# Transposing the attention probabilities as float32r from score buffers at a fixed place

## The chip, the cores and the metric

The kernel runs on one core of one Trainium2 chip. What counts is the device time of one execution in microseconds. Each number of the tables is the median of several executions; the rows of the trace come from one further, profiled execution.

## The reference

Four batches of eight heads, a sequence of 576, a head of 64, all in float32, followed by two feed-forward layers over 2304 tokens (512 to 2048 to 512):

```python
scores = scale * np.matmul(q, k.transpose(0, 1, 3, 2))
cum = np.cumsum(np.maximum(s, 0.0), axis=-1)
bias = -(cum[:, :, :, None] - cum[:, :, None, :])
scores = np.where(causal, -1000000000.0, scores + np.minimum(bias, 0.0))
attn = np.exp(scores - np.max(scores, axis=-1, keepdims=True))
attn = attn / (np.sum(attn, axis=-1, keepdims=True) + 1e-09)
x = np.matmul(attn, v)                  # then (tokens, heads * head_dim)
h = x @ w_in1;  x = np.maximum(0.01 * h, h) @ w_out1
h = x @ w_in2;  x = (np.maximum(h, 0.0) + np.log1p(np.exp(-np.abs(h)))) @ w_out2
```

The feed-forward weights come as float64 and are split in the kernel.

## The kernel before, in words

Three stages follow each other: attention (about the first 240 us) with a part of the first feed-forward layer woven in, the rest of the first layer, and the second layer. In both layers each float32 operand is split into two float32r tiles, a high and a low part, and a product is three float32r matmuls (lines 145, 635, 854, 1023, 1078, 1105).

Attention works on 16 pairs of heads. The 576 query rows of a pair are cut into units: the block of rows 384 to 511, a unit called "last" for the remaining 64 rows of both heads, the block of rows 256 to 383, and the two first blocks together. A unit passes through a pipeline, one step of the main loop behind the other:

- `scores`: TensorE multiplies Q and K in float32 and adds the decay bias through a second matmul of two rows (lines 302, 307, 316), into two PSUM tiles, j = 0 and 1 for the two heads;
- `maxima`: VectorE (DVE) adds the mask, finds the row extremes and writes the scores into `sc`, a tile of 128 x 2 x 512 float32 from a ring of three buffers (line 337);
- `exps`: ScalarE (ACT) takes the exponential in place and its row sums (line 349);
- `norm`: GpSimd (POOL) multiplies by the reciprocal of the sum in place (line 360);
- `transpose`: TensorE transposes each 128 columns of `sc` into a PSUM tile `pt_t`, with the identity `ident` as the streamed operand (lines 368, 372, 377). There are 20 transposes of line 377, four of line 372 and one of line 368 in a pair, 400 in all;
- `evacuate`: ACT or DVE copies `pt_t` to PA, PZ or PB (lines 389, 391);
- `pv`: TensorE multiplies by V in float32 (line 409).

In one step of the loop the unit n is at its maxima and exponentials, n - 1 at its norm, n - 2 at its transposes, and n - 3 at its last evacuation. From about 60 us on, each step also holds six matmuls of the first layer, put there by `fill.step`. The order of instructions on every engine is the order in which the program writes them.

Ahead of the loop stands the preparation: `masks()` and `make_identity(nc, ident)` write on POOL; `decay0()` then issues the loads of the first Q and K from ACT's queue, the loads of s and the later Q, K, V and weights from SP's queue, starts 18 warm-up matmuls on TensorE (`wake`, line 191), and computes the cumulative sums of s with ACT and DVE for the bias rows BK0 and BQ0 (lines 210 to 216).

SBUF is handed out by pools; those with `side="right"` grow from the right edge. At that edge stands `edge`, 24 floats; left of it come the pools of the woven-in layer (`Fill`), which are closed after attention.

Of the kernel before, what the change touches and what calls it, by code (L numbers as in the profile page):

```python
# [10 lines left out]
F32 = mybir.dt.float32  # L11
I32 = mybir.dt.int32
U32 = mybir.dt.uint32
F32R = mybir.dt.float32r
AF = mybir.ActivationFunctionType
# [3 lines left out]
P = 128  # L19
# [6 lines left out]
def view(t, offset, *dims):  # L26

    return bass.AP(t.tensor, t.offset + offset, [list(t.ap[0])] + [list(d) for d in dims])
# [3 lines left out]
def attn_moe_moe(ctx, tc, q, k, v, s, w1i, w1o, w2i, w2o, out):  # L32
    nc = tc.nc

    B, H, S = s.shape
# [8 lines left out]
    NB = S // P  # L44
    TL = S - NB * P
# [5 lines left out]
    def pool(name, bufs=1, **kw):  # L51
        return tc.tile_pool(name=name, bufs=bufs, **kw)
# [2 lines left out]
    keep = ctx.enter_context(pool("keep"))  # L55
    edge = ctx.enter_context(pool("edge", side="right"))
    edge.tile([P, 24], F32, tag="edge", name="edge")

    xh = keep.tile([P, KD, NT], F32R, tag="xh", name="xh")
    xl = keep.tile([P, KD, NT], F32R, tag="xl", name="xl")  # L60
# [11 lines left out]
    def tick():  # L72
        clock[0] += 1
        for fn, args in todo.pop(clock[0], ()):
            fn(*args)
# [78 lines left out]

    def attention(att, ps, fills):
        ident = att.tile([P, P], F32, tag="ident", name="ident")

# [14 lines left out]
        BK0, BQ0 = view(PB, 0, [1, S]), view(PB, S, [1, ZQ])  # L174
        c0, c1 = (view(PA, i * S, [1, S])[:BH] for i in range(2))
        one = view(V[1], 0, [1, S])
        s0, s1 = (view(att.tile([P, 2, 512], F32, tag="sc", name="sc", bufs=3), 0, [1, S]) for _ in range(2))
        base = att.tile([P, 12], F32, tag="st", name="st", bufs=4)[:, :1]

        def blank(i):  # L180
# [12 lines left out]
        def decay0():  # L193

            pitch = list(s1.ap[0])[0]
            nc.sync.dma_start(
                bass.AP(s1.tensor, s1.offset, [[D * pitch, 2], [1, S]]), bass.AP(s.tensor, s.offset, [[S, 2], [1, S]])
            )
            load(0, "q", nc.scalar)
            nc.sync.dma_start(c0, s.rearrange("b h s -> (b h) s"))  # L200
            load(0, "k", nc.scalar, slice(0, S))
            nc.vector.memset(one[:, :P], 1.0)
            wake(one[:, :P])
            nc.vector.memset(one[:, P:], 1.0)
            nc.vector.memset(base, 0.0)
            for j in range(2):
                nc.vector.memset(base[j * D + 32:j * D + 33], -1.0)
            for i in (1, 0):
                nc.vector.memset(BK[i].bitcast(F32), -1.0)
            nc.vector.tensor_scalar(s0[:1], s1[:1], 0.0, 1.0 / scale, op0=ALU.max, op1=ALU.mult)  # L210
            for y, x in ((s0[D:D + 1], s1[D:D + 1]), (c0, c0)):
                nc.scalar.activation(y, x, AF.Relu, scale=1.0 / scale)
            nc.vector.tensor_tensor_scan(BK0, one, s0, base, op0=ALU.mult, op1=ALU.add)
            nc.scalar.activation(BQ0[32:33, :S], BK0[:1], AF.Copy)
            for c, n, queue in ((slice(0, SB), 0, nc.vector), (slice(S, ZQ), SB, nc.gpsimd)):
                queue.tensor_copy(BQ0[D + 32:D + 33, c], BK0[D:D + 1, n:n + c.stop - c.start])
# [20 lines left out]
        def zeros():  # L237
            nc.gpsimd.memset(PZ[TL:], 0.0)
# [40 lines left out]
        class Unit:  # L279
# [43 lines left out]

            def maxima(self, j):
                if j == 0:
                    self.sc = att.tile([P, 2, 512], F32, tag="sc", name="sc", bufs=3)
                    self.st = att.tile([P, 12], F32, tag="st", name="st", bufs=4)
                    if self.last:
                        self.sc = view(self.sc, 0, [self.W, 2], [1, self.W])
                w = slice(0, self.W)  # L330
                ml = (mask[:, w], maskl)[j] if not self.p else M[self.p % 2][:, j * SH:(j + 1) * SH]
                todo = [(w, ml, j)] if self.last else [
                    (c, mask[:, (NB - 1 - t) * P:], j * len(self.subs) + i) for i, (t, c) in enumerate(self.subs)
                ]
                low = self.stat(0, 0) if self.last and j else 3.0e38
                for c, m, e in todo:
                    nc.vector.tensor_tensor_reduce(  # L337
                        out=self.sc[:, j, c], in0=self.ps[j][:, c], in1=m, scale=-scale, scalar=low,
                        op0=ALU.add, op1=ALU.min, accum_out=self.stat(0, e),
                    )  # L340
# [19 lines left out]
                    nc.gpsimd.tensor_scalar(x, x, self.stat(2, e), 1.0, op0=ALU.mult, op1=ALU.mult)  # L360

            def transpose(self, j):
                sc = self.sc
                pt = ps.tile([P, 512], F32, tag="t", name="pt_t", bufs=2)
                if self.last:
                    sc = view(sc, 0, [1, S])
                    if j:
                        nc.tensor.transpose(pt[:TL, :P], sc[:, NB * P:S], ident)
                        self.outs = PZ[:TL], pt[:TL, :P].rearrange("p (j x) -> p j x", x=TL)
                        return  # L370
                    for c in range(NB):
                        nc.tensor.transpose(pt[:, c * P:(c + 1) * P], sc[:, c * P:(c + 1) * P], ident)  # L372
                    self.outs = PA[:, :, :, P:], pt.rearrange("p (c j x) -> p j c x", j=2, x=TL)
                    return
                n = self.W // P
                for c in range(n):
                    nc.tensor.transpose(pt[:, c * P:(c + 1) * P], sc[:, j, c * P:(c + 1) * P], ident)  # L377
                src = pt[:, :self.W].rearrange("p (c x) -> p c x", x=P)
                if n == NB:
                    self.outs = PA[:, j, :, :P], src  # L380
                else:
                    k = len(self.subs)
                    self.outs = PB[:, j, :, (2 - k) * P:(3 - k) * P], src
# [45 lines left out]
        def masks():  # L429
            nc.gpsimd.memset(s0, 0.0)  # L430
            nc.gpsimd.memset(BQ0, 1.0)
            for j in range(2):
                nc.gpsimd.memset(BQ0[j * D:(j + 1) * D, NB * P + (1 - j) * TL:NB * P + (2 - j) * TL], 0.0)
            nc.gpsimd.memset(mask, 0.0)
            nc.gpsimd.memset(maskl, 0.0)
            d0 = (NB - 1) * P
            nc.gpsimd.affine_select(
                out=mask[:, d0:d0 + P], in_=mask[:, d0:d0 + P], compare_op=ALU.is_ge,
                fill=NEG, base=0, pattern=[[-1, P]], channel_multiplier=1,
            )  # L440
            for r in (0, TL):
                nc.gpsimd.affine_select(
                    out=maskl[r:r + TL, S // 2 - TL:], in_=maskl[r:r + TL, S // 2 - TL:], compare_op=ALU.is_ge,
                    fill=NEG, base=0, pattern=[[-1, TL]], channel_multiplier=1,
                )

        fill = fills()
        masks()
        make_identity(nc, ident)
        zeros()  # L450
        decay0()
        for i in (1, 0):
# [19 lines left out]
        for n in range(len(units) + 3):  # L472
            p, i = divmod(n, len(order))
# [185 lines left out]
    with pool("att") as att:  # L659
        attention(att, psA, make)  # L660
    fill = fills[0]
    while fill.units or fill.rest or todo:
        fill.run()
        tick()
    fill.stack.close()

    acc = ctx.enter_context(pool("accpool")).tile([P, KD, NT], F32, tag="acc", name="acc")
    stages = [ExitStack(), ExitStack()]
# [197 lines left out]
    def at(n, fn, *args):  # L866
        plan.setdefault(n, []).append((fn, args))
# [259 lines left out]
    for n, q in enumerate(quads):  # L1127
        q.at(t)
        if n + 1 < len(quads):
            j = quads[n + 1].sb, quads[n + 1].j  # L1130
# [86 lines left out]
```

## Time and profile before

| | us |
|---|---|
| median of 3 runs | 951.89 |
| lowest and highest | 951.88, 952.91 |
| the profiled execution | 951.81 |
| its span, first to last instruction | 950.0 |

| engine | busy us | share of the span | instructions |
|---|---|---|---|
| TensorE matmul (PE) | 941.3 | 99% | 5173 |
| TensorE weight load (PEld) | 767.3 | 81% | 5173 |
| VectorE (DVE) | 668.0 | 70% | 1294 |
| ScalarE (ACT) | 575.8 | 61% | 1185 |
| GpSimd (POOL) | 564.3 | 59% | 548 |

Matmuls are pipelined: a record of one holds its way through the array, so records of neighbours overlap, and the distance from start to start is what each adds. The loading of a matmul's stationary operand has a record of its own under PEld; in a transpose that is the block to be transposed. A chain is followed back from the last instruction to what released each step.

### The profile page before, as it was taken

Reading aid. Unit: us, or ns where it says so; the run is one execution under the profiler, and the core shown is the slowest. Engines: PE = TensorE matmul, PEld = TensorE weight load, DVE = VectorE, ACT = ScalarE, POOL = GpSimd, SP = SyncE. Lnnn points to the kernel's source line nnn. Section 1 sums busy time; section 2 is a strip of 40 time slices with the busy share of each in tenths; the row PEclk is TensorE's granted clock in tenths of the full one; section 3 lists DMA queues with packets and bytes.
Section 4 is the critical chain, followed back from the end, with each engine's and each line's share of the span. In section 5 each row is a group of like instructions: output and inputs, shape, how many; then the busy total and the mean of one; then the engine's idle time right before and its main releaser. Section 6 shows DMA issues by size and latency. Waiting matters only on the chain.

```text
span 950.0 us, 15346 instructions
## 1 busy us (share of the span) xinstructions
PE 941.3 (99%) x5173; PEld 767.3 (81%) x5173; DVE 668.0 (70%) x1294; ACT 575.8 (61%) x1185; POOL 564.3 (59%) x548
## 2 busy tenths in 40 slices
PE   9999999999999999999999999999999999999998
PEld 6666767777998888888888888888888888888887
DVE  8888656554479798778998745665666666766666
ACT  6888677665566564546555446666656765565563
POOL 7778556444367676657666534755654664555443
PEclk9999999999999999999999999999999999999999
DMA  7453434331665654546476244341415248445402
GB/s 248 148 164 127 144 111 134 119 106 37 215 239 180 229 190 139 173 166 213 132 269 217 102 151 159 115 136 66 153 65 177 89 150 314 135 136 175 134 0 90
DMA packets 79251, 143.61 MB, mean 151 GB/s; under 512 B 7626, under 2 KB 24906, under 8 KB 79172
## 3 DMA queue, kind: packets, MB, share of 16 engines
q1 hardware_dynamic: 78740, 141.87, 44.9%
q8 instruction: 41, 0.67, 0.3%
q10 hardware_dynamic: 432, 0.75, 0.3%
q14 instruction: 38, 0.31, 0.1%
HBM read 109.33 MB, written 33.25 MB: 150 GB/s over the span
## 4 chain that ended last, share of the span: by engine, by line
PE 93%; DVE 3%; POOL 1%; ACT 1%; issue 1%; DMA 0%; SPq 0%; DVEq 0%; POOLq 0%; ACTq 0%
PE ps_h L145 20%; PE ps_out L1078 20%; PE ps_out L854 17%; PE ps_h L1023 16%; PE pt_s L316 4%; PE pt_t L377 3%; PE ps_o L635 3%; PE pt_v L409 3%; PE ps_h L1105 2%; PE pt_s L409 1%; PE pt_t L372 1%; PE pt_s L302 1%; DVE sc L337 1%; POOL sc L360 0%; ACT sc L349 0%
## 5 line engine op out<-in xcount | busy, mean ns | idle before, releaser
L974 POOL TENSOR_TENSOR l<-l,e 128x512 f32<-128x512 f32 x72 | 93.5, 1298 | 161.8 <-DVE e L971 147.5
L151 POOL TENSOR_TENSOR gl<-gf,gh 128x512 fp32r<-128x512 f32 (+2 forms) x68 | 88.7, 1305 | 111.7 <-ACT gh L150 78.5
L360 POOL TENSOR_SCALAR sc<-sc,st 128x512 f32<-128x512 f32 (+4 forms) x160 | 88.4, 563 | 79.2 <-DVE st L356 61.3
L145 PE MATMUL ps_h<-xh,wih 128*128 128x512 f32 (+2 forms) x320 | 119.9, 375 | 0.0
L145 PE MATMUL ps_h<-xh,wil 128*128 128x512 f32 (+2 forms) x320 | 118.1, 369 | 0.0
L145 PE MATMUL ps_h<-xl,wih 128*128 128x512 f32 (+2 forms) x320 | 117.9, 368 | 0.0
L1086 DVE TENSOR_TENSOR acc<-ps_out,acc 128x512 f32<-128x512 f32 (+1 forms) x127 | 86.8, 685 | 42.5 <-PE ps_out L1078 40.0
L1078 PE MATMUL ps_out<-woh,gh 128*128 128x512 f32 x290 | 112.5, 388 | 0.8 <-DVE acc L1086 0.8
L1078 PE MATMUL ps_out<-wol,gh 128*128 128x512 f32 x290 | 112.4, 388 | 0.0
L349 ACT ACTIVATE sc<-sc,st 128x512 f32<-128x512 f32 (+2 forms) x144 | 83.4, 582 | 34.5 <-DVE st L337 28.7
L854 PE MATMUL ps_out<-gh,woh 128*128 128x512 f32 (+2 forms) x272 | 99.2, 365 | 0.3 <-DVE acc L861 0.3
L854 PE MATMUL ps_out<-gh,wol 128*128 128x512 f32 (+2 forms) x272 | 99.1, 364 | 0.0
L854 PE MATMUL ps_out<-gl,woh 128*128 128x512 f32 (+2 forms) x272 | 99.0, 364 | 0.0
L834 ACT ACTIVATE gf<-ps_h 128x512 f32<-128x512 f32 (+2 forms) x68 | 37.1, 546 | 101.4 <-PE ps_h L145 92.7
L984 POOL TENSOR_TENSOR gl<-l,gh 128x512 fp32r<-128x512 f32 x72 | 93.6, 1308 | 3.0 <-ACT gh L980 3.0
L1078 PE MATMUL ps_out<-woh,gl 128*128 128x512 f32 x290 | 88.9, 388 | 0.0
L980 ACT ACTIVATE gh<-l 128x512 fp32r<-128x512 f32 x72 | 45.4, 630 | 66.0 <-POOL l L974 66.0
L1023 PE MATMUL ps_h<-xh,wih 128*128 128x512 f32 x208 | 81.0, 389 | 0.0
L1023 PE MATMUL ps_h<-xl,wih 128*128 128x512 f32 x208 | 81.0, 389 | 0.0
L1023 PE MATMUL ps_h<-xh,wil 128*128 128x512 f32 x208 | 80.9, 389 | 0.0
L337 DVE CUSTOM_DVE_ANT_0 sc<-pt_s,mask 128x512 f32<-128x512 f32 (+3 forms) x129 | 59.2, 483 | 16.2 <-PE pt_t L377 15.4
L145 PEld LDWEIGHTS ps_h<-xh,wil 128*128 128x128 f32 x320 | 60.2, 188 | 9.6
(168 smaller groups left out, 2369.7 us busy)
## 6 DMA issues: line engine op xcount, KB each, us to landing
w2d<-stg SPq DMA_DIRECT2D x88, 256.0 KB
rawi<-in_moe_w_in SPq DMA_DIRECT2D x32, 512.0 KB
rawo<-in_moe_w_out SPq DMA_DIRECT2D x32, 512.0 KB
wih<-w2d SPq DMA_DIRECT2D x64, 256.0 KB
wil<-w2d SPq DMA_DIRECT2D x64, 256.0 KB
woh<-w2d SPq DMA_DIRECT2D x32, 256.0 KB
wol<-w2d SPq DMA_DIRECT2D x32, 256.0 KB
K<-in_k SPq DMA_DIRECT2D x15, 432.0 KB
```

Of the source, the lines that this page charges most:

```text
L145: nc.tensor.matmul(ps, a, b, start=kk == 0 and n == 0, stop=kk == KD - 1 and n == 2)
L151: nc.gpsimd.tensor_tensor(gl, gf, gh.bitcast(F32), op=ALU.subtract)
L337: nc.vector.tensor_tensor_reduce(out=self.sc[:, j, c], in0=self.ps[j][:, c], in1=m, scale=-scale, scalar=low, op0=ALU.add, op1=ALU.min, ac ...
L349: nc.scalar.activation(x, x, AF.Exp, scale=-1.0, bias=self.stat(0, e + self.last), accum_out=self.stat(1, e))
L360: nc.gpsimd.tensor_scalar(x, x, self.stat(2, e), 1.0, op0=ALU.mult, op1=ALU.mult)
L854: nc.tensor.matmul(ps, a, b, start=f == 0 and m == 0, stop=f == G - 1 and m == 2)
L974: nc.gpsimd.tensor_tensor(self.l, self.l, self.e, op=ALU.subtract)
L980: nc.scalar.activation(self.gh, self.l, AF.Copy)
L984: nc.gpsimd.tensor_tensor(self.gl, self.l, self.gh.bitcast(F32), op=ALU.subtract)
L1023: nc.tensor.matmul(self.ps[name], x, y, start=n < 4 and kp == 0 and m == 0, stop=kp == 1 and m == 2, skip_group_check=n >= 4,)
L1078: nc.tensor.matmul(u, a, v, start=m == 0, stop=m == len(ops) - 1)
L1086: nc.vector.tensor_tensor(d[..., w], o[..., w], d[..., w], op=ALU.add)
```

## The change

The three buffers of the `sc` ring are no longer pool tiles. A pool `arena` reserves their 12 KB per partition next to the right edge, and each buffer is addressed there under two names: `sc`, float32, for DVE, ACT and POOL, and `bits`, float32r, for the transposes. The identity gets a float32r copy, `turn`, made by ACT right behind `make_identity`, and the transposes write the PSUM tile as float32r. The arena is closed behind the pools of the woven-in layer.

```diff
+    arena = ExitStack()
+    arena.enter_context(pool("arena", side="right")).tile([P, 3, 2, 512], F32, tag="arena", name="arena")
+    low = (nc.sbuf_usable_end - 4 * 24) // P * P - 3 * 2 * 512 * 4
...
         ident = att.tile([P, P], F32, tag="ident", name="ident")
+        turn = att.tile([P, P], F32R, tag="turn", name="turn")
+        at = lambda nm, i, dt: nc.alloc_sbuf_tensor_at(f"{nm}{i}", [P, 2, 512], dt, offset=low + 4 * 1024 * i).ap()
+        scores = cycle([(at("sc", i, F32), at("bits", i, F32R)) for i in range(3)])
...
-        s0, s1 = (view(att.tile([P, 2, 512], F32, tag="sc", name="sc", bufs=3), 0, [1, S]) for _ in range(2))
+        s0, s1 = (view(next(scores)[0], 0, [1, S]) for _ in range(2))
...
                 if j == 0:
-                    self.sc = att.tile([P, 2, 512], F32, tag="sc", name="sc", bufs=3)
+                    self.sc, self.bits = next(scores)
...
             def transpose(self, j):
-                sc = self.sc
+                sc = self.bits
                 pt = ps.tile([P, 512], F32, tag="t", name="pt_t", bufs=2)
+                out = pt.bitcast(F32R)
                 if self.last:
                     sc = view(sc, 0, [1, S])
                     if j:
-                        nc.tensor.transpose(pt[:TL, :P], sc[:, NB * P:S], ident)
+                        nc.tensor.transpose(out[:TL, :P], sc[:, NB * P:S], turn)
...
                     for c in range(NB):
-                        nc.tensor.transpose(pt[:, c * P:(c + 1) * P], sc[:, c * P:(c + 1) * P], ident)
+                        nc.tensor.transpose(out[:, c * P:(c + 1) * P], sc[:, c * P:(c + 1) * P], turn)
...
                 for c in range(n):
-                    nc.tensor.transpose(pt[:, c * P:(c + 1) * P], sc[:, j, c * P:(c + 1) * P], ident)
+                    nc.tensor.transpose(out[:, c * P:(c + 1) * P], sc[:, j, c * P:(c + 1) * P], turn)
...
         masks()
         make_identity(nc, ident)
+        nc.scalar.activation(turn, ident, AF.Copy)
         zeros()
         decay0()
...
     fill.stack.close()
+    arena.close()
```

## Rows read from the trace of the kernel before

**Rows 1.** The page: span, then TensorE's busy time, share and instructions.

```profile
span 950.0 us, 15346 instructions
...
PE 941.3 (99%) x5173; PEld 767.3 (81%) x5173; DVE 668.0 (70%) x1294; ACT 575.8 (61%) x1185; POOL 564.3 (59%) x548
```

**Rows 2.** Busy time by stretch, 180 to 200 us; after POOL: granted clock, DMA share, GB/s.

```profile
180.00:200.00 20.00, 20.00 (x150) 14.11 (x150) 11.62 (x51) 12.46 (x37) 6.64 (x13) 1.00 0.29 98
```

**Rows 3.** The chain by line in four stretches: 5:24, 24:62, 62:100, 100:240 us.

```profile
by line: PE pt_s L316 34.2%; DMA K<-in_k 21.9%; POOL sc L360 7.4%; POOL wm L123 6.3%; PE pt_s L307 6.2%; PE pt_t L377 5.4%; SPq L247 5.1%; DVE sc L337 5.1%; issue 3.6%; PE pt_s L302 3.4%; DVE wm L120 3.2%; PE pt_t L372 3.1%; SPq L82 2.8%; D
...
by line: PE pt_s L316 24.8%; PE pt_v L409 19.4%; PE pt_t L377 17.7%; POOL wil L133 6.6%; PE pt_t L372 6.3%; POOL sc L360 4.9%; issue 4.1%; PE ps_h L145 3.7%; DVE PA L391 3.6%; DVE sc L337 3.1%; PE pt_s L302 1.7%; POOL M L75 1.5%; DVE st L35
...
by line: PE ps_h L145 26.2%; PE pt_s L316 18.9%; PE pt_t L377 16.1%; PE pt_v L409 15.9%; PE ps_o L635 3.7%; PE pt_s L302 3.4%; POOL wol L133 3.3%; PE pt_t L372 3.1%; DVE st L355 2.1%; DVE PA L391 1.8%; issue 1.8%; DVE sc L337 1.6%; POOL sc 
...
by line: PE ps_o L635 18.0%; PE ps_h L145 13.9%; PE pt_s L316 13.8%; PE pt_t L377 12.3%; PE pt_v L409 9.6%; PE pt_s L409 8.9%; PE pt_t L372 3.8%; PE pt_s L302 3.7%; ACT sc L349 3.1%; DVE sc L337 3.0%; issue 2.1%; DVE xl L420 1.5%; POOL wm L
```

**Rows 4.** The chain through one head pair: start us, us, what.

```profile
177.71 0.59 PE pt_t L377 x4
178.30 1.39 PE ps_o L635 x6
179.68 0.44 PE pt_t L377 x4
...
183.38 0.11 PE pt_t L368
...
187.00 0.48 PE pt_t L377 x3
...
188.87 0.66 PE pt_t L377 x6
...
190.91 0.33 PE pt_t L377 x3
```

**Rows 5.** Matmuls by line and shape: count, busy us, mean ns of one record, idle us.

```profile
L1078 PE MATMUL ps_out<-wol,gh 128*128 128x512 f32 x286 | 111.3, 389 | 0.0
...
L1105 PE MATMUL ps_h<-xh,wil 128*128 128x256 f32 x64 | 18.1, 283 | 0.0
...
L409 PE MATMUL pt_v<-PB,V 128*64 128x128 f32 x128 | 12.8, 279 | 0.0
...
L191 PE MATMUL pt_w<-V 128*128 128x128 f32 x18 | 4.2, 430 | 1.0 <-DVE V L202 1.0
```

**Rows 6.** Loads of the stationary operand by line and shape, columns as above.

```profile
L145 PEld LDWEIGHTS ps_h<-xh,wil 128*128 128x128 f32 x320 | 60.2, 188 | 9.6
...
L377 PEld LDWEIGHTS pt_t<-ident,sc 128*128 128x128 f32 x320 | 36.2, 140 | 16.3 <-POOL sc L360 4.3 <-issue 2.8 <-POOL wol L133 0.9
...
L409 PEld LDWEIGHTS pt_v<-PB,V 128*64 128x64 f32 x256 | 15.9, 137 | 6.3 <-issue 1.7
...
L368 PEld LDWEIGHTS pt_t<-ident,sc 128*64 128x64 f32 x16 | 1.8, 110 | 0.5
```

**Rows 7.** POOL in order of time, the second step on ident: start us, us.

```profile
4.38 1.28 POOL masks.py:199 TENSOR_SCALAR_AFFINE_SELECT ident<-ident 128x128 f32<-128x128 f32 x1
```

**Rows 8.** ACT's queue in order of time, the start.

```profile
0.76 0.38 ACTq L247 DMA_DIRECT2D Q<-in_q  x1
1.17 0.45 ACTq L247 DMA_DIRECT2D K<-in_k  x1
```

**Rows 9.** TensorE in order of time at the start, then the chain there.

```profile
1.04 4.21 PE L191 MATMUL pt_w<-V 128*128 128x128 f32 x18 [1.04 <-DVE V L202]
5.47 1.36 PE L316 MATMUL pt_s<-K,Q 64*128 64x512 f32 x4 [0.21 <-DMA K<-in_k]
...
1.17 4.16 DMA K<-in_k
...
5.47 2.22 PE pt_s L316 x8
```

**Rows 10.** Busy time by stretch, 8 to 10 us; columns as in rows 2.

```profile
8.00:10.00 2.00, 2.00 (x16) 1.12 (x10) 2.00 (x6) 1.80 (x5) 1.79 (x6) 1.00 1.04 387
```

**Rows 11.** Waits of attention: engine and line, releaser, us, times, longest us.

```profile
PEld pt_t L377 <- POOL sc L360: 4.3, 12, 0.6
```

## The prediction

> **What bounds the kernel now.** The page first: TensorE (PE) is busy 99% of the span [rows 1], and the granted clock of an attention stretch is 1.00, the higher level, 2.4 GHz [rows 2]. So time taken from TensorE inside attention can shorten the whole, but only where TensorE is what the next step waits for. For that I read the chain of waits, summed by line, over the four parts of attention [rows 3]. The reader is to see two things. The transposes (pt_t, lines 377 and 372) are on the chain everywhere: 8.5% of 19 us, 24.0% of 38 us, 19.2% of 38 us and 16.1% of 140 us, which is 1.6 + 9.1 + 7.3 + 22.5 = 40.5 us. And the first part has another entry, the load of K, with 21.9%: the start hangs on a transfer, not on TensorE.
>
> How much of all transposing is on the chain? One undisturbed head pair shows its seven groups: 0.59 (and a second group like it, line 372), 0.44, 0.11, 0.48, 0.66 and 0.33 us [rows 4], 3.20 us for 25 transposes; 16 pairs give 51.2 us for 400. So 40.5 of 51.2, or 79%: 316 of the 400 transposes lie where their length counts.
>
> **The change, part by part.**
>
> *The transposes.* Six in a row take 0.66 us, 110 ns each [rows 4]. Two things could set that pace: loading the block to be transposed, and streaming the 128 columns of the identity. The matmuls on float32r tiles give the stream: a record of 512 columns is 389 ns and one of 256 columns 283 ns [rows 5], so a column costs 0.41 ns and 128 columns 53 ns; 110 ns is two such passes. The load of a transpose record shrinks from 140 ns for 128 columns to 110 ns for 64 [rows 6], so 128 columns take 60 ns, which fits beneath the 110 ns. The float32 transpose is therefore set by its two streaming passes. As float32r it should stream once, 53 ns. Then the load sets the pace, and here the trace has no row for the new form: if it loads as the float32 transpose does, 60 ns; if it loads as the float32r weights do, whose records shrink from 188 ns for 128 columns to 137 ns for 64 (a float32 load of the same kind) [rows 6], 102 ns. So the gain lies between 50 and 8 ns for each; if the second pass stays, it is nothing. The two nearest rows pull opposite ways (the same operation, or the same type), so I take the middle, 81 ns, a gain of 29 ns. On the chain: 316 x 29 = 9.2 us. Some of it is lost where another engine is close behind, as the twelve waits of the transposes for POOL's normalisation show (4.3 us) [rows 11]; I keep 8.0 us. The ends: 316 x 50 x 0.87 = 13.7 us and 2.5 us, or nothing.
>
> The Trainium skill ("TensorE: Matmul & The Clock Gate", section "Back-to-back issue gap") gives about 81 ns for a weight load and a 128-column matmul in a stream, and about 131 ns at 512 columns; the trace's six 512-column matmuls in 1.39 us [rows 4] are 232 ns each, so the page does not hold here at the larger size, and at 128 columns no run here shows it yet. By it the chain would lose 316 x 29 ns, the same as the middle that I took from the rows.
>
> *The new identity.* One copy of 128x128 on ACT. Its own length is small; its place is what counts. It is written directly behind the building of ident and ahead of decay0, and ACT works its queue in order. The instruction that it waits for, POOL's second step on ident, runs from 4.38 us for 1.28 us, to 5.66 us [rows 7]. Queued on ACT behind the copy are the loads of the first Q and K, which in the kernel before were issued at 0.76 and 1.17 us [rows 8], then the Relus of the decay and the copy for BQ0. TensorE's first scores wait for K: issue at 1.17 us, 4.16 us to landing, scores at 5.47 us [rows 9]. After: the copy starts at about 5.75 us, the Q issue beside or just behind it, K's issue 0.41 us later, at 6.2 us; K lands at 10.3 us at the earliest, and the scores start at about 10.5 us, 5.0 us later. The Relus and the BQ0 copy slip too, but they have the 4 us in which K travels, so they are hidden by it. DVE, POOL and ACT cannot use the time: their attention work is in order behind these scores. So nothing covers the delay, and what starts at 5.47 us moves as a block.
>
> Two additions. In the old place Q and K had a head start on SP's loads; in the new one they meet them, and the DMA engines are full then (share 1.04 from 8 to 10 us) [rows 10]. If they only get their part of it, K comes up to about 1.2 us later; I take 0.5. And the warm-up matmuls, 18 from 1.04 us for 4.21 us [rows 9], no longer touch the scores: TensorE stands idle from 5.25 to 10.5 us. The warm-up runs 18 matmuls of 128 columns at 430 ns a record, where the later float32 ones of 128 columns take 279 ns [rows 5]; 4.21 us over 18 is twice the 110 ns of two passes, the lower level, 1.2 GHz, and before it TensorE had done nothing. If it is back there when the scores come, the chain's work of the next 4 to 5 us, which begins with 2.22 us of scores on TensorE [rows 9], costs up to 2.5 us more. No row of before shows TensorE idle for 5 us, so the ends are 0 and 2.5; I take 1.5.
>
> The Trainium skill (same page, section "What's actually happening") says that the low clock is the default and activity lifts it, so an idle stretch of this kind would cost; no row of before has one. By it alone the start would cost 7.5 to 8.0 us in place of the 5.5 without a clock loss.
>
> Start: 5.0 + 0.5 + 1.5 = 7.0 us, with ends 5.0 and 8.7.
>
> *The fixed place and the two names.* The same three buffers of 4 KB; no instruction is added or removed by it. The arena sits at the right edge until attention is over, so the pools of the next stage take other addresses. I cost this at nothing: in the attention stretches PE has work queued, and the last transposes are read long before that stage writes there. What could cost: TensorE now reads another name than POOL writes, so a transpose of the first half might wait for the whole buffer (below).
>
> **Sum.** The profiled execution: 951.81 us with a span of 950.0, at the median of the three runs (951.89). 951.8 + 7.0 - 8.0 = 950.8 us.
>
> **The rivals.**
>
> *One streaming pass and the short load (B).* For it: the load row of the very same operation, 60 ns [rows 6]. Against: that row is of the other type. 951.8 + 7.0 - 13.7 = 945.1 us.
>
> *The load of float32r sets the pace (C), on the slower side.* For it: every 128-column float32r load in the trace is 188 ns against the transposes' 140 [rows 6]. Place: each transposing group; price: the gain shrinks to 2.5 us or to nothing, and the start remains. 951.8 + 7.0 - 2.5 = 956.3, to 958.8 us. It decides from a spacing of about 95 ns up, where 316 x 15 x 0.87 = 4 us no longer covers the start.
>
> *The loads are not delayed (D).* If the copy does not stand ahead of them on ACT, the start term falls away: 951.8 - 8.0 = 943.8 us. Against: the loads are the first instructions of ACT's queue now, and the copy is written ahead of them.
>
> *The two names make transposes wait for both halves (E).* The longest such wait now is 0.6 us [rows 11]; it would come where POOL is late. With 5 us over 64 units: about 955.8 us. For it only that the reader's name is another one.
>
> **How the numbers follow.** The forecast (A), 950.8 with its own range of 947 to 954 us, has 0.45; B 0.20; C 0.25; D 0.05; E 0.05. A change under 0.2% (1.9 us, 950.0 to 953.8) can't be told from none in this kernel. Faster: B and D whole and a third of A, 0.40. Slower: C and E and an eighth of A, 0.35. The same: the rest of A, 0.25. The range has to reach B's 945 and C's 958: 943.5 to 958.5 us; outside are the far ends of B, C and D, under 0.2.
>
> **What would show it.** In the trace after: ACT's first work behind the table load is the copy, at about 5.75 us, with the loads of Q and K issued behind it, and the first scores at 10.5 to 11.5 us instead of 5.47; the first scores' records longer than before if the clock fell. Transposes in a row at 81 ns (A), 60 ns (B), 102 to 110 ns (C); their load records at 140 ns or at 188. Attention shorter by 8 us from first score to last. The later stages as long as before. Wrong would make it: a spacing outside 70 to 95 ns, a start that is hidden, or transposes with longer waits for POOL.

## The result, and the profile after

| | us |
|---|---|
| the changed kernel, median of 4 runs | 962.19 (960.77 to 963.04) |
| the kernel before on the same chip, median of 4 runs | 952.37 |
| ratio, 95% interval | 1.0102 (1.0084 to 1.0119) |
| the profiled execution, and its span | 960.77, 959.0 |

The change makes the kernel 1.0% slower, some 9.7 us. The prediction said 950.8 us with a range of 943.5 to 958.5, so the time moved the other way and lies outside the range.

The page after: span, TensorE's busy time, the granted clock in 40 slices, and the chain that ended last by engine.

```profile
span 959.0 us, 15300 instructions
...
PE 934.4 (97%) x5173; PEld 763.6 (80%) x5173; DVE 670.0 (70%) x1294; ACT 575.5 (60%) x1186; POOL 563.8 (59%) x548
...
PEclk7999999999999999999999999999999999999999
...
PE 85%; DVE 5%; POOL 3%; ACT 2%; DMA 2%; issue 1%; SPq 0%; DVEq 0%; ACTq 0%; POOLq 0%
```

The last of these lines in the kernel before:

```profile
PE 93%; DVE 3%; POOL 1%; ACT 1%; issue 1%; DMA 0%; SPq 0%; DVEq 0%; POOLq 0%; ACTq 0%
```

Against [rows 1] TensorE is busy 6.9 us less, as the change should make it, but the span is 9.0 us longer: there are 15.9 us more in which TensorE has nothing to do, and its share of the chain falls from 93% to 85%. The clock row, all 9 in later slices, begins with a 7, so the first slice of 24 us is one place to look.

The start, in order of time (start us, us, what): POOL's second step on ident and the ACT queue behind it, then two steps of the chain, then TensorE. The last two lines are of the kernel before: DVE's scan beside POOL's step, and its first transposes.

```profile
4.41 0.29 POOL masks.py:199 TENSOR_SCALAR_AFFINE_SELECT ident<-ident 128x128 f32<-128x128 f32 x1
4.73 0.31 ACT L457 ACTIVATE turn<-ident 128x128 fp32r<-128x128 f32 x1 [2.73 <-POOL ident masks.py:199]
4.74 0.38 ACTq L253 DMA_DIRECT2D Q<-in_q  x1
5.16 0.49 ACTq L253 DMA_DIRECT2D K<-in_k  x1
```
```profile
5.16 7.29 DMA K<-in_k
12.58 3.79 PE pt_s L322 x8
```
```profile
1.04 4.11 PE L197 MATMUL pt_w<-V 128*128 128x128 f32 x18 [1.04 <-DVE V L208]
12.58 2.08 PE L322 MATMUL pt_s<-K,Q 64*128 64x512 f32 x4 [7.43 <-DMA K<-in_k]
...
22.34 0.87 PE L384 MATMUL pt_t<-turn,bits 128*128 128x128 f32 x8
```
```profile
4.15 1.42 DVE L213 TENSOR_TENSOR_SCAN PB<-V,st,sc 128x576 f32<-128x576 f32 x1 [0.21 <-ACT sc L212]
...
12.60 1.09 PE L377 MATMUL pt_t<-ident,sc 128*128 128x128 f32 x8
```

K is issued at 5.16 us where it was issued at 1.17 [rows 8], and its transfer takes 7.29 us where it took 4.16 [rows 9]: 4.0 and 3.1 us. TensorE is idle for 7.43 us. Then its work from the first scores to the first transposes takes 22.34 - 12.58 = 9.76 us; before, the first transposes began at 12.60 and the scores at 5.47 [rows 9], 7.13 us. That is 2.6 us more for the same matmuls. Together the first transposes are 9.7 us late.

POOL's step on ident took 1.28 us before [rows 7] and takes 0.29 here. Before, DVE's scan ran beside it. Here the scan waits for ACT's Relu, which stands behind the copy, and comes later. In the traces of all twelve kernels the step takes 1.00 to 1.31 us where the scan runs beside it and 0.29 where it doesn't.

The windows there (columns as in rows 2).

```profile
6.00:8.00 2.00, 0.00 (x0) 0.00 (x0) 1.49 (x2) 1.20 (x3) 0.02 (x1) 1.00 0.99 366
8.00:10.00 2.00, 0.00 (x0) 0.00 (x0) 1.70 (x2) 0.72 (x2) 1.84 (x4) 0.58 1.04 373
...
12.00:18.00 6.00, 5.42 (x17) 2.08 (x18) 1.52 (x5) 0.79 (x3) 0.33 (x2) 0.50 0.01 3
18.00:20.00 2.00, 2.00 (x10) 1.11 (x10) 1.62 (x7) 0.73 (x3) 0.26 (x1) 0.86 0.01 2
20.00:22.00 2.00, 2.00 (x19) 1.32 (x17) 1.01 (x7) 0.96 (x3) 1.10 (x2) 1.00 0.44 113
```

The granted clock falls to 0.50, the lower level, while TensorE stands idle (it is 1.00 from 6 to 8 us, 0.58 in the next slice) and comes back within the slice from 18 to 20 us, which reads 0.86; the scores run at half pace until then. The DMA share beside it is 0.99 to 1.04: the engines are full while K is on its way.

The transposes: first their tile's records by shape (min/median/max ns, first and last start), with the line of what its engine sat idle for (us, times), that line in the kernel before, then the wait that answers to [rows 11].

```profile
L384 PEld LDWEIGHTS pt_t<-turn,bits x320: 137/140/146, 22.3 to 243.0; 128*128 128x128 f32 x160
L384 PE MATMUL pt_t<-turn,bits x320: 220/249/284, 22.3 to 243.1; 128*128 128x128 f32 x160
...
  POOL sc L366: 23.6, 33
```
```profile
  POOL sc L360: 8.4, 21
```
```profile
PEld pt_t L384 <- POOL sc L366: 13.5, 18, 1.9
```

The load of a transpose is still 140 ns, as in [rows 6]. The records of line 384 that follow each other start 86 ns apart (the median of 248 pairs of records; within a group the distances go from about 60 to 116 ns). The same pairs of the kernel before have a median of 109. So the gain is there. But the transposes now wait for POOL's normalisation 18 times, 13.5 us and up to 1.9 us long, where line 377 waited 12 times, 4.3 us and at most 0.6 [rows 11]; for all transposing lines and both of TensorE's queues it is 23.6 us in 33 waits, where it was 8.4 in 21.

### The profile page after: what moved, and what is told of

Same layout as the page of the kernel before. It is cut to its first block, busy times and chain, and to the rows that moved or that the text cites. A ratio compares the mean times of both kernels' runs of the same rounds, so it can differ in the third digit from the quotient of the medians.

```text
span 959.0 us, 15300 instructions
## 1 busy us (share of the span) xinstructions
PE 934.4 (97%) x5173; PEld 763.6 (80%) x5173; DVE 670.0 (70%) x1294; ACT 575.5 (60%) x1186; POOL 563.8 (59%) x548
## 4 chain that ended last, share of the span: by engine, by line
PE 85%; DVE 5%; POOL 3%; ACT 2%; DMA 2%; issue 1%; SPq 0%; DVEq 0%; ACTq 0%; POOLq 0%
PE ps_out L1087 20%; PE ps_h L148 18%; PE ps_out L863 16%; PE ps_h L1032 16%; PE pt_s L322 3%; PE ps_o L643 3%; PE ps_h L1114 2%; PE pt_t L384 2%; PE pt_v L416 2%; PE pt_s L416 1%; POOL sc L366 1%; DVE sc L343 1%; ACT sc L355 1%; DMA K<-in_k 1%; PE pt_s L308 1%
```

## The experiments

Three causes compete: the start (queue, transfer and clock), the two names (a transpose waits for more of POOL's work than it reads), and the fixed place. The first four kernels ran on one chip beside the kernel before (952.02 us, 25 runs), the next four on one (952.04 us, 13 runs), the last two on one (952.06 us, 7 runs). In brackets behind a time stand the lowest and the highest, behind a ratio its 95% interval; the interval is some 0.9 us to each side for the kernels run ten times, and 1.4 to 1.7 us for those run four times.

### The copy of the identity later: the start alone

```diff
         make_identity(nc, ident)
-        nc.scalar.activation(turn, ident, AF.Copy)
         zeros()
         decay0()
+        nc.scalar.activation(turn, ident, AF.Copy)
```

> The changed kernel with one line moved: the copy of the identity on ACT stands behind decay0, so the loads of Q and K and the Relus are ahead of it again. Theory start (the copy held the loads back, and the delay passed through whole): first scores at 5.5 us again, the clock steady, and 962.2 less the 9.7 us by which the first transposes were late, 952.5 us (951.5 to 953.5). Rival (the late start only hides other waits that take its place): 956 us or more, with the start early all the same.

Measured: 951.63 us (10 runs), ratio 0.9997 (0.9988 to 1.0007). Against the changed kernel's 1.0102 that is 1.05% or 10.0 us, by one line's place. The first scores of this kernel:

```profile
5.18 1.46 PE L322 MATMUL pt_s<-K,Q 64*128 64x512 f32 x4
```

Its first transposes start at 12.59 us, as in the kernel before. The start is as large as the whole of the loss; but without it the kernel only equals the one before, so something else eats the transposes' gain.

### Two names, both float32: the names without the gain

```diff
-        turn = att.tile([P, P], F32R, tag="turn", name="turn")
+        turn = ident
-        scores = cycle([(at("sc", i, F32), at("bits", i, F32R)) for i in range(3)])
+        scores = cycle([(at("sc", i, F32), at("bits", i, F32)) for i in range(3)])
...
-                out = pt.bitcast(F32R)
+                out = pt
...
-        nc.scalar.activation(turn, ident, AF.Copy)
```

The transposes stream `ident` as in the kernel before, and there is no second identity.

> The changed kernel with float32 in both names, the old identity and no copy on ACT: fixed place and two names alone. Transposes at 110 ns again. Theory names (the reader's other name makes each unit's transposes wait for both halves of the normalisation): one wait of the transposes for POOL in each unit, 64 in all, where before had 160; slower than before by what the gain in attention fell short of, some 5 us, so 957 us (955 to 959). Rival (the names cost nothing, the gain is lost because TensorE is off the path): 952.4 to 953.5 us.

Measured: 956.82 us, ratio 1.0048 (1.0033 to 1.0063). Nothing but a second name and a place, and 956.82 - 952.02 = 4.8 us are lost. Counted from the semaphore events in the trace, the loads of pt_t wait for POOL at 64 places, one for each unit; in the kernel before there are 160, one for each part that POOL finishes.

### One name, float32, fixed place: the place alone

The other lines are those of the run above.

```diff
-        scores = cycle([(at("sc", i, F32), at("bits", i, F32R)) for i in range(3)])
+        scores = cycle([(x, x) for x in (at("sc", i, F32) for i in range(3))])
```

> As the run with two float32 names, but the transposes read the writers' name: the fixed place alone. Theory names: 160 waits again and 952.4 us, as before; if the step of 1.2 us behind attention comes from the arena's place, 953.6 us. Rival (the place, not the names, brings the coarser waits): as slow as with two names, 957 us.

Measured: 952.99 us, ratio 1.0008 (0.9998 to 1.0017). The 160 waits are back, so the second name and not the place costs 956.82 - 952.99 = 3.8 us. What is left is about 1 us, which the interval of the ratio alone doesn't tell from nothing; the trace puts most of it (0.9 us) at the end of attention. SP's queue there, in this kernel: three loads of raw weights, then the wait of their line (us, times, longest us).

```profile
246.59 1.48 SPq L96 DMA_DIRECT2D rawi<-in_moe_w_in  x3
```
```profile
SPq L96 <- DMA part<-o: 1.5, 1, 1.5
```

These loads wait for DMAs that read `o`, a tile of the woven-in layer. The arena moved the layer's pools 12 KB to the left, and the weights of the next stage now land on them.

### Names for each block: too fine on the wrong side

```diff
-        scores = cycle([(at("sc", i, F32), at("bits", i, F32R)) for i in range(3)])
+        part = lambda i, c: nc.alloc_sbuf_tensor_at(f"bits{i}{c}", [P, P], F32R, offset=low + 4 * 1024 * i + 4 * P * c).ap()
+        scores = cycle([(at("sc", i, F32), [part(i, c) for c in range(8)]) for i in range(3)])
...
-                    nc.tensor.transpose(out[:, c * P:(c + 1) * P], sc[:, j, c * P:(c + 1) * P], turn)
+                    nc.tensor.transpose(out[:, c * P:(c + 1) * P], sc[4 * j + c], turn)
```

The readers' name is split into one for each 128 columns, the writers' name covers the whole buffer. The copy of the identity is late, as in the first run.

> The changed kernel with the copy behind decay0, and one float32r name for each 128 columns of a buffer instead of one for all 1024. Theory names: if the waits go by the name that is read, each block of transposes waits only for the half that it reads, 160 waits again, and the float32r gain comes through: 952.5 less 5, 947 us (945 to 949). If the other name is matched to the writers' whole buffer, 64 waits and the time of the run with the copy moved, 952.5 us. Rival (TensorE off the path): 952.5 us even with 160 waits.

Measured: 951.63 us, ratio 0.9998 (0.9989 to 1.0008), and still 64 waits. Splitting the readers' name changes nothing: the wait is for the writers' last write to the whole of the writers' name.

### Names for each half, of writers and readers

```diff
-        at = lambda nm, i, dt: nc.alloc_sbuf_tensor_at(f"{nm}{i}", [P, 2, 512], dt, offset=low + 4 * 1024 * i).ap()
-        scores = cycle([(at("sc", i, F32), at("bits", i, F32R)) for i in range(3)])
+        at = lambda nm, i, dt, n=512, j=0: nc.alloc_sbuf_tensor_at(f"{nm}{i}{j}", [P, n], dt, offset=low + 4 * (1024 * i + 512 * j)).ap()
+        scores = cycle([(*([at(nm, i, dt, 512, j) for j in range(2)] for nm, dt in (("sc", F32), ("bits", F32R))),
+                         at("sl", i, F32, S), at("bl", i, F32R, S)) for i in range(3)])
...
```

The two names of 576 columns are for the unit called last. The lines left out make each step use the name of its half. The copy of the identity is late.

> The copy of the identity stands behind decay0, as in the run with it late (951.63 us, ratio 0.9997), and each buffer now has a writers' name and a readers' name for each half of 512 columns (and a pair of 576 columns for the unit called last) in place of one pair for both halves. Names theory (a transpose through the readers' name waits for the writers' last writes to the whole of the writers' name): the loads of pt_t wait for POOL at two places in a unit again, more than 100 of them in place of 64, the 4.6 us that the run with two float32 names showed are back, and the time is 951.6 - 4.6 = 947.0 us (945 to 949). Rival (the waits are hidden by the work of the woven-in layer and the missing gain is that TensorE's shorter transposes lie off the path): 951.6 us.

Measured: 947.16 us (946.82 to 947.74), ratio 0.9947 (0.9932 to 0.9962), with 112 waits for POOL. The names theory holds and the rival falls: TensorE's shorter transposes are on the path. The wait that answers to [rows 11], in this kernel, and what all its transposes sat idle for:

```profile
PEld pt_t L385 <- POOL sc L368: 4.5, 12, 0.9
```
```profile
  POOL sc L368: 10.7, 23
```

It is 4.5 us in 12 waits, the size that it had before the change, where the changed kernel has 13.5 us in 18; over all transposes 10.7 us in 23 waits, against 23.6 in 33.

Where the names cost shows in the distance from one pair's first transposes of the unit called last to the next pair's (line 379 with the copy late, line 380 here). Over the 15 distances it is 4.2 us, and 2.3 of them lie in two: 16.72 against 15.32 us and 14.15 against 13.21, from 76 to 107 us. The last three distances are 14.82, 14.82 and 14.29 us with the copy late and 14.81, 14.82 and 14.30 here: there the names cost nothing.

### The other order of two pools: the place

```diff
-                self.gpool, self.tpool = new("gpoolA", G + 1), new("tpoolA", 2)
+                self.tpool, self.gpool = new("tpoolA", 2), new("gpoolA", G + 1)
```

Once on top of the names by half, once on top of one float32 name.

> As the names by half, and the two pools of the woven-in layer that lie next to the arena are opened in the other order, so that the raw weights' place in the next stage falls on other tiles. Place theory (the step of about 1.2 us at the end of attention is the raw weights' load waiting for the o tiles that now lie where it lands): the step is gone, 947.0 - 1.2 = 945.8 us. Rival (the step is the arena's later release or comes from elsewhere): 947.0 us. Where the other order puts the load onto tiles that are read still later: above 947.0 us.

> Fixed place, one name, float32, no second identity (952.99 us, ratio 1.0008), and the two pools of the woven-in layer in the other order. Place theory: the step at the end of attention is gone and the time is that of the kernel before, 952.0 us. Rival: 953.0 us.

Measured: 946.28 us, ratio 0.9940 (0.9925 to 0.9955), and 952.01 us, ratio 1.0000 (0.9991 to 1.0010): 0.9 and 1.0 us less than without the swap. Each of these differences is inside the intervals of the two ratios that it is taken from; the traces have to carry it. SP's loads of raw weights at the end of attention, first of the kernel before, then of the second of these two:

```profile
244.67 1.53 SPq L93 DMA_DIRECT2D rawi<-in_moe_w_in  x3
```
```profile
244.75 1.53 SPq L96 DMA_DIRECT2D rawi<-in_moe_w_in  x3
```

In the kernel with the place alone they were at 246.59 us, and in the float32r pair they go from 240.62 to 238.93. The wait for `o` is no longer among SP's waits in either, the profiled spans are 1.0 and 1.1 us shorter, and the float32 kernel runs as the one before. So the place costs about 1 us through the tiles that the next loads land on. The first of the two kernels beats both the kernel before, by 5.7 us, and the changed one.

### SP's loads after the decay rows: the transfer

```diff
         fill.step(-2)
-        load(1, "q")
-        load(1, "k")
         fill.step(-1)
-        load(0, "v")
...
                 parts()
+                load(0, "v")
+                load(1, "q")
+                load(1, "k")
```

> The changed kernel with SP's early loads of the next Q, the next K and the first V moved behind the moves of the decay rows, so that the first K, issued at 5.2 us, meets only the raw weights on the DMA engines. Contention theory (the transfer of K took 7.3 in place of 4.2 us because those loads fill the DMA engines): K lands in 4.2 to 5.5 us, the scores start at about 10 us in place of 12.6, and the time is 962.2 - 2 to 3 = 959.5 us (959 to 960.5), or less if the clock falls for a shorter time. Rival (the transfer is long because of its own queue, or the decay rows come last anyway): K lands at 12.4 us and the time stays at 962.

Measured: 965.55 us, ratio 1.0141 (1.0124 to 1.0158): the time went the wrong way. The profiled execution was the fastest of the four, 962.39 us; the other three took 965.28 to 965.92, so its trace shows the kind of loss and not its whole size. The chain of this kernel, its first transposes, and a window:

```profile
5.15 4.55 DMA K<-in_k
9.84 3.70 PE pt_s L322 x8
...
19.01 4.94 DMA K<-in_k
24.04 2.50 PE pt_s L322 x6
```
```profile
18.42 0.87 PE L384 MATMUL pt_t<-turn,bits 128*128 128x128 f32 x8
```
```profile
24.00:26.00 2.00, 1.96 (x6) 0.90 (x6) 0.00 (x0) 0.00 (x0) 0.00 (x0) 0.50 1.09 287
```

The first K travels 4.55 us in place of 7.29, issued at the same time, and the first transposes start at 18.42 us in place of 22.34: contention was what made it late. Of these 3.9 us the transfer is 2.7; the rest is work at half pace that ends sooner. But the next K, now issued at 19.01 us, keeps TensorE waiting in turn, and the clock falls there (0.50 from 24 to 30 us). The expected total was wrong, the reason for the transfer right.

### The same loads between the two halves of the decay rows

```diff
             for e, x in enumerate((hi, lo)):
                 for t, r in ((BK[1], e), (BQ[1], 32 + e)):
                     ...
+                if e == 0:
+                    load(1, "k")
+                    load(1, "q")
+                    load(0, "v")
...
```

> The changed kernel with SP's loads of the next K and Q and the first V placed between the two halves of the decay rows' moves, behind the first K's transfer and some 7 us earlier than in the run that put them behind all of the moves, where the next K was issued at 19.0 us and TensorE waited for it. Contention theory: the first K lands in 4.6 us as in that run, the first transposes start at about 18.5 us in place of 22.3, the next K is there in time, and the span is 959.0 - 3.8 = 955.2 us (954.5 to 956.5). Rival (what the first K gains the next one loses wherever the loads stand): the scores of the second pair wait for K again, and the span is 958 us or more.

Measured: 959.05 us (958.67 to 959.46), ratio 1.0070 (1.0053 to 1.0087): against the changed kernel's 1.0102 that is 3.0 us.

```profile
5.16 4.42 DMA K<-in_k
```
```profile
18.93 0.88 PE L388 MATMUL pt_t<-turn,bits 128*128 128x128 f32 x8
```

The first K takes 4.42 us and the first transposes start at 18.93 us, 3.4 earlier; the next K is in time. The span, 957.5 us, misses the 955.2 that was expected. Part of the miss is that the expectation started from the span of the changed kernel's profiled execution, the fastest of its four; by the medians 3.0 us are gained where 3.8 were expected. The trace tells of the rest: pair by pair, the transposes of the unit called last start 3.4 us earlier than in the changed kernel up to 98.5 us, 1.8 earlier at 114.3, and 1.2 earlier from 143.8 us on. The windows of this kernel, then those of the changed one at the same work:

```profile
102.00:104.00 2.00, 1.52 (x9) 1.11 (x7) 1.25 (x4) 1.15 (x4) 2.00 (x3) 1.00 0.76 210
104.00:106.00 2.00, 0.72 (x5) 0.68 (x6) 1.52 (x8) 0.49 (x3) 1.92 (x6) 1.00 0.53 178
106.00:108.00 2.00, 2.00 (x11) 1.45 (x11) 0.10 (x1) 1.46 (x4) 0.67 (x1) 0.67 0.01 4
108.00:110.00 2.00, 2.00 (x10) 1.31 (x12) 0.89 (x4) 0.16 (x1) 0.98 (x2) 0.50 0.35 131
```
```profile
106.00:108.00 2.00, 0.96 (x7) 0.64 (x5) 0.99 (x4) 1.41 (x4) 2.00 (x4) 1.00 0.85 246
108.00:110.00 2.00, 1.31 (x8) 1.15 (x9) 1.20 (x7) 0.82 (x2) 1.92 (x4) 1.00 0.19 61
110.00:112.00 2.00, 2.00 (x18) 1.51 (x16) 0.94 (x4) 1.02 (x3) 0.23 (x2) 1.00 0.00 0
```

TensorE is idle for 1.8 us of the four from 102 to 106, nearly all of it one wait of the transposes for POOL, and then the clock is 0.67 and 0.50 in the next two slices. The changed kernel is idle for 1.7 us of four at the same work (106 to 110 us), and its clock stays at 1.00. So this is another fall of the clock, and it answers to the first 1.6 us that are lost again. To the other 0.6 answers a wait of 0.5 us for a later K, between 130 and 150 us, which the changed kernel doesn't have. All this is one profiled execution. The mean granted clock of the four executions is 0.994, 0.994, 0.998 and 1.000, and the two with the higher clock are only 0.6 us faster than the profiled one. So this fall of the clock doesn't explain the times of all four, and what the others lost stays open.

### A longer warm-up: the clock

```diff
-            for i in range(9):
+            for i in range(42):
```

Each of these float32 matmuls is two records in the trace: 18 records for 9, 84 for 42.

> The changed kernel with 42 warm-up matmuls in place of 9, so that TensorE is at work until K lands at about 12.4 us. The numbers are those of the profiled execution (span). Clock theory (2.6 us of the longer start are the lower clock, which fell while TensorE stood idle from 5.2 to 12.6 us): the granted clock stays at 1.00 up to the first transposes, these start at 22.3 - 2.6 = 19.7 us (19.5 to 20.4), and the span is 959.0 - 2.6 = 956.4 us. Rival (the first scores are slow for another reason, the decay rows for one): first transposes at 22 us or later, span 959 us.

Measured: 958.80 us, ratio 1.0069 (1.0054 to 1.0084), span 956.9 us. TensorE in order of time:

```profile
1.04 12.23 PE L197 MATMUL pt_w<-V 128*128 128x128 f32 x84 [1.04 <-DVE V L208]
13.37 1.13 PE L322 MATMUL pt_s<-K,Q 64*128 64x512 f32 x4
...
20.28 0.88 PE L384 MATMUL pt_t<-turn,bits 128*128 128x128 f32 x8
```

The granted clock reads 1.00 in every slice of the start, and the first scores take 1.13 us where they took 2.08. From scores to transposes there are 6.91 us against 9.76. The warm-up runs on for 0.8 us past the time at which the scores could start, so 2.1 of the 2.9 us are gained in this trace; by the medians it is 3.1 us against the changed kernel's 1.0102. The clock theory holds.

## Why the prediction was wrong

By the runs, the 9.7 us are made up of the start, 10.0 us (the copy late against the change); the names, 951.63 - 947.16 = 4.5 us; the place, 947.16 - 946.28 = 0.9 us; and a gain by the transposes of 952.01 - 946.28 = 5.7 us (one name against float32r names by half, both with the pools swapped). 10.0 + 4.5 + 0.9 - 5.7 = 9.7. The sum closes because each term is the difference of two neighbouring kernels, so its closing proves nothing; each term is uncertain by some two us. The prediction had 7.0 + 0 + 0 - 8.0.

- **The step that failed is "the fixed place and the two names: I cost this at nothing".** Its last sentence named the right mechanism, a transpose that waits for the whole buffer, and the rival E priced it at 5 us; 4.5 were measured. But I gave it a chance of 0.05, for it spoke only that the name is another. What the trace of before did show was that a pipeline step has little room: 12 waits of line 377 on POOL, up to 0.6 us each [rows 11]. Waiting for both halves makes those waits longer: up to 1.9 us, 13.5 in all. The place was costed at nothing too, with the reason that the last transposes are read long before the next stage writes there. That looked at the wrong tiles: it was `o`, moved by the arena, that was still being read (0.9 us).
- **The start was mis-sized: 7.0 us taken, with ends 5.0 and 8.7; 9.7 in the trace, 10.0 in the runs.** The queue was 4.0, not 5.0: POOL's step on ident, priced at 1.28 us from [rows 7], took 0.29, since the scan that ran beside it was itself held back, so K was issued at 5.16 and not 6.2. The transfer was 3.1 us longer, not 0.5 (my bound was 1.2): the two runs that move SP's loads out of K's way give 4.4 to 4.6 us for the same K. [Rows 10] showed full DMA engines from 8 to 10 us; the mistake was to count K's share of them as nearly the whole. The clock took 2.6 us, not 1.5, a little past my end of 2.5.
- **The transposes: 81 ns taken, 86 measured, with the load still at 140 ns.** The number is near, but by luck: by the prediction's own working a load of 140 ns allows 60 ns for each transpose (B), and 86 is neither that nor the 102 of C. What sets the 86 ns stays open; B and C fall as prices. Two slips in its sums: the lower end of the gain is 316 x 8 x 0.87 = 2.2 us, not 2.5, and the gain no longer covers a start of 7.0 us from a spacing of about 85 ns up, not 95. At 24 ns the sum is 316 x 24 x 0.87 = 6.6 us in place of 8.0; measured are 5.7. The remaining 0.9 us is a question of how much lies on the chain. In the float32 kernel with the swapped pools a late pair takes 15.37 us from one group of line 379 to the next, in the float32r one (line 380) 14.82: 0.55 us or 22 ns for each of its 25 transposes. But the first four periods, up to 60 us, together get only 0.6 us shorter, where four times 0.55 would be 2.2. There the transposes were on the chain by line [rows 3], but shortening them hands part of the place to another engine: from 14 to 60 us their share of the chain falls from 19.8% to 10.7% between these two kernels, and that of POOL's normalisation rises from 7.4% to 10.2%.
- **The rival D** (loads not delayed, 943.8 us) is the run with the copy late: 951.6. With the names, the place and the 2.3 us of gain that were overestimated it is 943.8 + 4.5 + 0.9 + 2.3 = 951.5; that is the sum above once more, not a check of it.

Of the full DMA engines in [rows 10] and in the windows after: the two runs that took SP's loads away from K shortened its transfer although K stayed on ACT's queue and they on SP's. The Trainium skill ("DMA: Bandwidth & Descriptors", section "Issuing engines are not separate DMA queues") says that transfers begun by different engines run on the same 16 DMA engines and interleave; these runs agree (7.29 against 4.55 and 4.42 us).

Of the clock the prediction quoted the Trainium skill ("TensorE: Matmul & The Clock Gate", section "What's actually happening"): low by default, lifted by activity. The run with the longer warm-up agrees: 1.00 in every slice of the start and 6.91 us, against a fall to 0.50 and 9.76 us. The 81 ns that the Trainium skill gives for a stream of 128-column matmuls (same page, section "Back-to-back issue gap") lie near the 86 ns here.

## What to carry to other kernels

A second name for a buffer is a dependency of its own: name what is written and read together, in pieces that match the pipeline's steps (here a half), or the readers wait for all of the writers. A helper instruction on an engine's queue costs what stands behind it: look for loads there before placing it, and for the loads of other queues that the delayed one will then meet. And when a reservation moves other pools, look at whose tiles the next stage's first loads land on.

## What the runs showed of the hardware that was not expected

- The granted clock of the profile reads 1.00 from the start, but the warm-up matmuls do not run at that pace: 213 ns from start to start. In the run with 84 of them it changes to 112 ns at 6.5 us; in the run with the loads between, at 4.3 us already. The trace's own record of the clock begins at 6.51 and at 4.29 us in these two: before its first record the profile shows 1.00. The windows of the run with 84, of the warm-up matmuls alone, show it in the counts of 2 us each (busy time and count of the matmuls, then of their loads, granted clock, DMA share, GB/s):

```profile
3.00:5.00 2.00, 2.00 (x11) 2.00 (x11) 1.00 0.85 227
5.00:7.00 2.00, 2.00 (x14) 2.00 (x13) 1.00 1.04 369
7.00:9.00 2.00, 2.00 (x21) 2.00 (x20) 1.00 0.99 340
```

- So a row of 1.00 near the start does not say that the engine is at the higher level: pace has to be read from the records. In the run with SP's loads after the decay rows the clock row is 1.00 from 6 to 14 us, and yet the first scores take 2.08 us, at half pace; its record of the clock begins at 13.25 us. So in that execution the clock didn't fall in the idle stretch: it had not yet risen. In the kernel before the record begins at 5.98 us, behind the start of the first scores (5.47), and their first four records take 1.36 us where the run with the longer warm-up has 1.13.
- Two traces of the same work differ in whether the clock falls: the run with the loads between shows 0.67 and 0.50 from 106 to 110 us behind 1.8 us of idle time, the changed kernel 1.00 behind 1.7 us. What decides there stays open.
